# Issuing a retention-and-routing kernel in a hand-written order instead of by the automatic scheduler

## The chip, the cores and the metric

One Trainium2 chip, one of its cores. The metric is the device time of one execution in microseconds, lower is better. A core has TensorE (PE: matrix products and transposes into PSUM), VectorE (DVE), ScalarE (ACT), GpSimd (POOL), SyncE (SP, here only the issuer of transfers), and DMA engines that all of them share. Each engine runs its own instruction queue in order; semaphores between the queues carry the dependencies.

## The reference

Eight batches of eight-head retention (attention with a decay instead of a softmax) over 576 positions, then a layer in which each of the 4608 tokens goes to one of eight experts.

```python
def _attn_ref(q, k, v):                      # (8, 8, 576, 64) each
    scores = scale * np.matmul(q, k.transpose(0, 1, 3, 2))
    gamma = 1.0 - 2.0 ** (-5.0 - np.arange(H))
    Dmat = np.where(rel >= 0, gamma[:, None, None] ** rel[None], 0.0)   # rel = query - key position
    return np.matmul(scores * Dmat[None], v)

def _moe_ref(x, w_gate, w1, w2):             # x (4608, 512), w1 (8, 512, 1024), w2 (8, 1024, 512)
    logits = x @ w_gate
    expert_idx = np.argmax(logits, axis=1)
    gate_w = softmax(logits)[np.arange(N), expert_idx]
    for e in range(E):
        mask = expert_idx == e
        out[mask] = gate_w[mask, None] * (np.maximum(x[mask] @ w1[e], 0.0) @ w2[e])
```

## The kernel before

**Attention stage.** The work is cut into 40 blocks (`blocks`, a batch and a chunk): five per batch, four of 128 positions and a short one of 64. Decay is folded into q and k, so that a block needs only a causal mask, and what earlier chunks contribute is a running state. `load_batch` (L80) fetches q, k and v of a whole batch into tiles of two buffers. For each block TensorE does `stage_S` (L251: states from k and v), `stage_SC` (L281: scores, then the mask product `sc` on DVE, L305), `stage_R` of the block before (L356: transposes of the result back into rows, a cast `xr` on ACT, a store into the DRAM tensor `x_rows` by SP), `stage_TK` of the next block (L236: k scaled on POOL into `kk`, then transposed), `stage_AV` (L309: result into `psx`, copied out by ACT as `xo` and DVE as `xT`), and, one a block, `stage_TQ` for the next batch (L220: q scaled on POOL into `qq`, then transposed). `stage_L1` and `stage_L2` (L372, L386) make the routing logits once a batch.

**Routing.** `softmax_top1`, `ranks`, `prep`, `rows_hot` and `place` (L404 to L528) pick each token's expert, rank the tokens of each expert, and build lists of token numbers per expert (`slots`). They are mostly short DVE instructions. They run in two phases: phase 0 after half of the tokens, in the attention stage; phase 1 after all.

**Expert stage.** A unit is an expert and a phase: 256 token rows (two blocks of 128) in phase 0, 384 (three blocks) in phase 1. `seq` (L601) lists the 16 units. For a unit, `gather` (L530) has POOL issue an indirect transfer per block that reads rows of `x_rows` into `xg` (six buffers); `trans` (L605) transposes them; `mm1` (L616) multiplies with w1 into `ht`; `mm2` (L632) multiplies with w2, scales the result on DVE into `ys` (four buffers), and has POOL scatter a block of rows to the output by an indirect transfer (L643). All scatters write the one output tensor. Weights come as float32 in 512 KB parts, eight an expert, through three staging tiles `wst`, and are cast to bfloat16 by DVE or ACT (`load_w`, L199); an expert's weights have three buffers.

**Order.** The text traces the program in loops (L553 and L660). The automatic scheduler then orders each engine's instructions by a model of their times. Only TensorE's instructions are held to the text's order, by `pin` (L54), which `mm` (L58) uses too; POOL, DVE, ACT and SP get theirs from the scheduler. After the experts comes a branch for tokens that did not fit the lists; it isn't taken here.

Of the kernel before, what the change touches and what calls it, by code (L numbers as in the profile page):

```python
# [10 lines left out]
ALU = mybir.AluOpType  # L11
# [7 lines left out]
P = 128  # L19
# [19 lines left out]
def kernel(  # L39
# [14 lines left out]
    def pin(i):  # L54
        tc.keep_in_program_order(i)
        return i

    def mm(out, lhsT, rhs, start, stop):  # L58
        return pin(nc.tensor.matmul(out=out, lhsT=lhsT, rhs=rhs, start=start, stop=stop,  # L59
                                    skip_group_check=True))  # L60
# [7 lines left out]
    stpool = ctx.enter_context(tc.tile_pool(name="wstage", bufs=3))  # L68
# [4 lines left out]
    ldp = p1.enter_context(tc.tile_pool(name="ld", bufs=2))  # L73
    wkp = p1.enter_context(tc.tile_pool(name="wk", bufs=2))
    wk1 = p1.enter_context(tc.tile_pool(name="wk1", bufs=1))
    attc = p1.enter_context(tc.tile_pool(name="attc", bufs=1))
    ps1 = p1.enter_context(tc.tile_pool(name="ps1", bufs=1, space=PSUM))


    def load_batch(b, first):  # L80


        qt = ldp.tile([P, H, NCH, DH], F32, tag="q", name="qt")
        kt = ldp.tile([P, NCH, H, DH], F32, tag="k", name="kt")
        vt = ldp.tile([P, NCH, H, DH], F32, tag="v", name="vt")
        qk = ldp.tile([P, H, DH], F32, tag="qkr", name="qk")
        vr = ldp.tile([P, H // 2, DH], F32, tag="vr", name="vr")
        for c in range(NCH):
            nc.sync.dma_start(out=kt[:, c, :, :], in_=k[b, :, c * P:(c + 1) * P, :].rearrange("h p d -> p h d"))
            if first:  # L90
                nc.sync.dma_start(out=qt[:, 2 * c:2 * c + 2, :, :],
                                  in_=q[b, 2 * c:2 * c + 2, 0:NCH * P, :].rearrange("h (p s) d -> p h s d", p=P))
            elif c == 0:
                nc.sync.dma_start(out=qt[:, :, :, :],
                                  in_=q[b, :, 0:NCH * P, :].rearrange("h (p s) d -> p h s d", p=P))
            nc.sync.dma_start(out=vt[:, c, :, :], in_=v[b, :, c * P:(c + 1) * P, :].rearrange("h p d -> p h d"))
        nc.sync.dma_start(out=qk[0:REM, :, :], in_=q[b, :, NCH * P:S, :].rearrange("h p d -> p h d"))
        nc.sync.dma_start(out=qk[REM:P, :, :], in_=k[b, :, NCH * P:S, :].rearrange("h p d -> p h d"))
        for j in range(2):
            nc.sync.dma_start(out=vr[j * REM:(j + 1) * REM, :, :],  # L100
                              in_=v[b, 4 * j:4 * j + 4, NCH * P:S, :].rearrange("h p d -> p h d"))
        return qt, kt, vt, qk, vr

    loads = {0: load_batch(0, True)}
# [4 lines left out]

    tri = attc.tile([P, REM], F32, name="tri")  # L110
    nc.gpsimd.memset(tri[:, :], 1.0)
    for j in range(2):
        nc.gpsimd.affine_select(out=tri[j * REM:(j + 1) * REM, :], in_=tri[j * REM:(j + 1) * REM, :],
                                pattern=[[1, REM]], base=0, channel_multiplier=-1,
                                compare_op=ALU.is_ge, fill=0.0)
    wgp = attc.tile([P, NP, 32], F32, name="wgp")
    nc.gpsimd.memset(wgp[:, :, :], 0.0)
    nc.sync.dma_start(out=wgp[:, :, 0:E], in_=moe_w_gate.rearrange("(c p) e -> p c e", p=P))

# [33 lines left out]
    nc.vector.tensor_copy(out=kg[0:REM, NCH, :], in_=qg[0:REM, NCH, :])  # L153
    zst = attc.tile([P, NP, DH], F32, name="zst")
    nc.gpsimd.memset(zst[:, :, :], 0.0)
# [3 lines left out]
    pss = ps1.tile([P, 2, 512], F32, name="pss")  # L159

# [34 lines left out]

    wb = {}
    casts = [nc.scalar.copy, nc.vector.tensor_copy, nc.gpsimd.tensor_copy]

    def load_w(e, part, eng):  # L199

        if e not in wb:
            wb[e] = (wpool.tile([P, NPT, F], BF16, tag="w1", name="w1b"),
                     wpool.tile([P, NFB, DM], BF16, tag="w2", name="w2b"))
        w1b, w2b = wb[e]
        st = stpool.tile([P, F], F32, tag="st", name="wst")
        c = part % 4
        if part < 4:
            nc.sync.dma_start(out=st[:, :], in_=moe_w1[e, c * P:(c + 1) * P, :])
            casts[eng](out=w1b[:, c, :], in_=st[:, :])
        else:  # L210
            nc.sync.dma_start(out=st[:, :].rearrange("p (s d) -> p s d", d=DM),
                              in_=moe_w2[e, c * 2 * P:(c + 1) * 2 * P, :].rearrange("(s p) d -> p s d", p=P))
            casts[eng](out=w2b[:, 2 * c:2 * c + 2, :], in_=st[:, :].rearrange("p (s d) -> p s d", d=DM))  # L213

    qTs, kTs, kks, scs, sts, xTs, lts = {}, {}, {}, {}, {}, {}, {}

    def stage_TQ(b, p):  # L220

        qt = loads[b][0]
        h0 = 2 * p
        qq = wkp.tile([P, NCH, P], F32, tag="qq")
        nc.gpsimd.tensor_tensor(  # L225
            out=qq[:, :, :].rearrange("p s (h d) -> p h s d", d=DH), in0=qt[:, h0:h0 + 2, :, :],
            in1=qg[:, 0:NCH, h0:h0 + 2].rearrange("p s h -> p h s").unsqueeze(3)
                .to_broadcast([P, 2, NCH, DH]), op=ALU.mult)
        pst = ps1.tile([P, 512], F32, tag="T", name="psq")
        for s_ in range(NCH):  # L230
            pin(nc.tensor.transpose(out=pst[:, s_:512:NCH], in_=qq[:, s_, :], identity=ident[:, :]))  # L231
        if b not in qTs:
            qTs[b] = wkp.tile([P, NP, 512], F32, tag="qT", name="qT")
        nc.scalar.copy(out=qTs[b][:, p, :], in_=pst[:, :])

    def stage_TK(b, c):  # L236
        kt, qk = loads[b][1], loads[b][3]
        kk = wkp.tile([P, H, DH], F32, tag="kk")
        nc.gpsimd.tensor_tensor(out=kk[:, :, :], in0=(kt[:, c, :, :] if c < NCH else qk[:, :, :]),  # L239
                                in1=kg[:, c, :].unsqueeze(2).to_broadcast([P, H, DH]), op=ALU.mult)  # L240
        pst = ps1.tile([P, 512], F32, tag="T", name="psk")
        for p in range(NP):
            pin(nc.tensor.transpose(out=pst[:, p * P:(p + 1) * P],
                                    in_=kk[:, 2 * p:2 * p + 2, :].rearrange("p h d -> p (h d)"),
                                    identity=ident[:, :]))
        kT = wkp.tile([P, NP, P], F32, tag="kT")
        nc.scalar.copy(out=kT[:, :, :].rearrange("p a t -> p (a t)"), in_=pst[:, :])
        kTs[(b, c)] = kT
        kks[(b, c)] = kk

    def stage_S(b, c):  # L251

        if c == NCH:
            return
        kk, vt = kks.pop((b, c)), loads[b][2]
        for p in range(NP):
            for par in range(2):
                r = slice(par * DH, (par + 1) * DH)
                for j in range(2):
                    h = 2 * p + j  # L260
                    mm(pss[j * DH:(j + 1) * DH, par, p * DH:(p + 1) * DH], kk[r, h, :], vt[r, c, h, :],
                       c == 0 and p == 0, c == NCH - 1)
        so = wkp.tile([P, NP, DH], F32, tag="so")
        e_, o_ = pss[:, 0, 0:NP * DH], pss[:, 1, 0:NP * DH]
        fl = so[:, :, :].rearrange("p a d -> p (a d)")
        if c == 0:
            nc.vector.tensor_copy(out=fl, in_=e_)
        else:

            nc.vector.tensor_tensor(out=fl, in0=e_, in1=sts[(b, c, "oo")][:, :, :].rearrange("p a d -> p (a d)"),  # L270
                                    op=ALU.add)
        so2 = wkp.tile([P, NP, DH], F32, tag="so2")
        nc.scalar.copy(out=so2[:, :, :].rearrange("p a d -> p (a d)"), in_=o_)
        se = wkp.tile([P, NP, DH], F32, tag="se")
        nc.vector.tensor_tensor(out=se[:, :, :].rearrange("p a d -> p (a d)"), in0=e_,
                                in1=so2[:, :, :].rearrange("p a d -> p (a d)"), op=ALU.add)
        sts[(b, c, 1)] = so
        sts[(b, c + 1, "oo")] = so2
        sts[(b, c + 1, 0)] = se

    def stage_SC(b, c):  # L281
        kT = kTs.pop((b, c))
        ps = ps1.tile([P, 2, 512], F32, tag="SC", name="pssc")
        sc = wkp.tile([P, 2, NP, DH], F32, tag="sc")
        scs[(b, c)] = sc
        if c < NCH:
# [22 lines left out]
    def stage_AV(b, c):  # L309
# [37 lines left out]
        if c < NCH:  # L347
            if c == 0:
                xTs[b] = wk1.tile([P, NCH, NP, P], F32, tag="xT", name="xT")
# [434 lines left out]
```

## Time and profile before

| | |
|---|---|
| time, median of 14 runs | 468.58 us (463.47 to 476.95) |
| time of the profiled execution | 464.41 us |
| its span | 462.7 us, granted TensorE clock 0.925 |
| busy TensorE, VectorE, ScalarE, GpSimd | 346.0, 182.7, 175.6, 164.4 us |
| moved by DMA | 82.31 MB, 178 GB/s over the span |
| last transposes of the routing logits | 245.4 us |
| first and last scatter start | 256.2 and 449.8 us |

A span is what the profile covers of one execution, the time includes what lies around it. The busy tenths below are the span in 40 slices of 11.6 us: TensorE, POOL, the DMA engines, and what they moved in GB/s. The attention stage is the first 21 slices, the expert stage the rest.

```profile
PE   1678879897766778776867778989495978999700
...
POOL 7254332524233163231100364133325344643220
...
DMA  9988878988887597887010135998556674222110
GB/s 213 244 184 217 188 197 202 247 216 209 214 222 194 163 261 193 231 294 239 20 38 7 55 115 189 323 308 264 202 209 215 243 248 137 91 82 91 67 69 14
```

A timeline line has: start, duration, engine, line of the kernel, operation, what it writes and reads, how many of them; in square brackets, how long the engine had been idle before and what ended that. A line of the waits has: who waited for whom, total us, how often, the longest.

### The profile page before, as it was taken

The numbers are of one execution on the slowest core, as the hardware profiler recorded it, in microseconds if no ns is written. First come the engines' busy times: TensorE is split into PE (matmuls) and PEld (weight loads), VectorE is DVE, ScalarE is ACT, GpSimd is POOL, SyncE is SP. The second block draws the span as 40 slices with busy tenths as digits, with TensorE's granted clock in tenths as the row PEclk, the third lists the DMA queues.
The fourth block names the chain that finished last, engine by engine and source line by source line (L and its number), as shares of the span: only waits on it lengthen the run. The fifth ranks groups of instructions, "written<-read, shape, count | busy, mean of one in ns | idle before, by whom it ended". The sixth has DMA issues, their size and how long they took to land. (4 is left out here: it accounts for less than half of the span.)

```text
span 462.7 us, 14452 instructions
## 1 busy us (share of the span) xinstructions
PE 346.0 (75%) x6306; PEld 256.0 (55%) x6322; DVE 182.7 (39%) x436; ACT 175.6 (38%) x316; POOL 164.4 (36%) x198
## 2 busy tenths in 40 slices
PE   1678879897766778776867778989495978999700
PEld 1567768786656667665755544556254544656300
DVE  2134423433387933344448724444233324323200
ACT  2245434545563366564432014445142323232200
POOL 7254332524233163231100364133325344643220
PEclk9999989999999879998999799999798898999955
DMA  9988878988887597887010135998556674222110
GB/s 213 244 184 217 188 197 202 247 216 209 214 222 194 163 261 193 231 294 239 20 38 7 55 115 189 323 308 264 202 209 215 243 248 137 91 82 91 67 69 14
DMA packets 112008, 82.31 MB, mean 178 GB/s; under 512 B 83262, under 2 KB 96062, under 8 KB 111936
## 3 DMA queue, kind: packets, MB, share of 16 engines
q1 hardware_dynamic: 106816, 66.61, 51.7%
q0 software_dynamic: 5120, 14.69, 9.0%
q8 instruction: 51, 0.84, 0.7%
q14 instruction: 21, 0.17, 0.1%
HBM read 67.13 MB, written 15.20 MB: 178 GB/s over the span
## 5 line engine op out<-in xcount | busy, mean ns | idle before, releaser
L643 POOL DMA_INDIRECT out_dram<-ys,tids x40 | 42.5, 1062 | 126.0 <-issue 46.1
L629 ACT ACTIVATE ht<-pm 128x384 bf16<-128x384 f32 (+1 forms) x96 | 49.3, 526 | 91.1 <-PE pm L59 79.6
L59 PE MATMUL pm<-xt,w1b 128*128 128x256 bf16 (+1 forms) x512 | 75.0, 306 | 4.1 <-ACT ht L629 2.7
L59 PE MATMUL py<-w2b,ht 128*128 128x512 bf16 x304 | 73.0, 396 | 1.4 <-issue 0.7
L59 PEld LDWEIGHTS <-w1b 128*128 128x128 bf16 x512 | 51.3, 100 | 27.4 <-issue 4.9
L225 POOL TENSOR_TENSOR qq<-qt,qg 128x512 f32<-128x512 f32 x32 | 34.2, 1074 | 87.7 <-PE psq L231 60.9
L642 DVE TENSOR_SCALAR ys<-py,gat 128x512 f32<-128x512 f32 x40 | 29.8, 749 | 66.9 <-DMA out_dram<-ys,tids 40.8
L59 PEld LDWEIGHTS <-ht 128*128 128x128 bf16 x320 | 32.1, 102 | 37.9 <-issue 6.7
L239 POOL TENSOR_TENSOR kk<-kt,kg 128x512 f32<-128x512 f32 x32 | 33.6, 1050 | 49.2 <-issue 30.3
L536 POOL DMA_INDIRECT xg<-x_rows,tidg x40 | 41.6, 1041 | 19.1 <-issue 9.0
L354 DVE TENSOR_TENSOR xT<-psx,xo 128x512 f32<-128x512 f32 x32 | 22.1, 690 | 63.4 <-ACT xo L346 63.4
L346 ACT COPY xo<-psx 128x512 f32<-128x512 f32 (+1 forms) x40 | 21.8, 544 | 51.9 <-PE psx L59 51.9
L59 PE MATMUL psx<-sc,vt 64*64 64x64 f32 x1024 | 23.2, 230 | 18.2 <-DVE sc L305 15.9
L59 PE MATMUL psx<-qT,so 64*64 64x64 f32 x512 | 34.8, 225 | 2.1 <-issue 2.1
L231 PE MATMUL psq<-ident,qq 128*128 128x128 f32 x128 | 23.3, 309 | 14.5 <-POOL qq L225 13.2
L59 PEld LDWEIGHTS psx<-sc,vt 64*64 64x64 f32 x1024 | 18.8, 140 | 24.9 <-DVE sc L305 20.6
L366 PE MATMUL psr<-ident,xT 128*128 128x128 f32 x128 | 21.9, 295 | 12.6 <-DVE xT L354 12.6
L612 PE MATMUL pt<-identb,xg 128*128 128x128 bf16 x160 | 13.8, 225 | 22.4 <-DVE xt L613 19.3
L59 PEld LDWEIGHTS psx<-qT,so 64*64 64x64 f32 x512 | 29.3, 141 | 0.9 <-issue 0.9
L213 ACT CAST w2b<-wst 128x1024 bf16<-128x1024 f32 x16 | 16.7, 1048 | 33.0 <-DMA wst<-in_moe_w_dram 33.0
L368 ACT CAST xr<-psr 128x512 bf16<-128x512 f32 (+1 forms) x40 | 23.4, 584 | 15.3 <-PE psr L366 15.2
L59 PE MATMUL pss<-vt,kk 64*64 64x64 f32 x1024 | 25.6, 236 | 2.2 <-issue 2.1
(124 smaller groups left out, 519.6 us busy)
## 6 DMA issues: line engine op xcount, KB each, us to landing
wst<-in_moe_w_dram SPq DMA_DIRECT2D x64, 512.0 KB
kt<-in_k_dram SPq DMA_DIRECT2D x32, 256.0 KB
vt<-in_v_dram SPq DMA_DIRECT2D x32, 256.0 KB
qt<-in_q_dram SPq DMA_DIRECT2D x7, 1024.0 KB
x_rows<-xr SPq DMA_DIRECT2D x32, 128.0 KB
qt<-in_q_dram SPq DMA_DIRECT2D x4, 256.0 KB
qk<-in_q_dram SPq DMA_DIRECT2D x8, 128.0 KB
qk<-in_k_dram SPq DMA_DIRECT2D x8, 128.0 KB
```

The costliest lines, as they stand in the source:

```text
L59: return pin(nc.tensor.matmul(out=out, lhsT=lhsT, rhs=rhs, start=start, stop=stop, skip_group_check=True))
L225: nc.gpsimd.tensor_tensor(out=qq[:, :, :].rearrange("p s (h d) -> p h s d", d=DH), in0=qt[:, h0:h0 + 2, :, :], in1=qg[:, 0:NCH, h0:h0 + 2] ...
L231: pin(nc.tensor.transpose(out=pst[:, s_:512:NCH], in_=qq[:, s_, :], identity=ident[:, :]))
L239: nc.gpsimd.tensor_tensor(out=kk[:, :, :], in0=(kt[:, c, :, :] if c < NCH else qk[:, :, :]), in1=kg[:, c, :].unsqueeze(2).to_broadcast([P, ...
L346: nc.scalar.copy(out=xo[:, :], in_=psx[:, 1, 0:n * P])
L354: nc.vector.tensor_tensor(out=dst, in0=psx[:, 0, 0:n * P], in1=xo[:, :], op=ALU.add)
L366: pin(nc.tensor.transpose(out=ps[0:n, p * P:(p + 1) * P], in_=src, identity=ident[:, :]))
L368: nc.scalar.copy(out=xr[0:n, :], in_=ps[0:n, :])
L536: nc.gpsimd.indirect_dma_start(out=xg[:, :], out_offset=None, in_=x_rows[0:nr, :], in_offset=bass.IndirectOffsetOnAxis(ap=slots[ph][1][:, ...
L629: nc.scalar.activation(out=ht[:, f0:f0 + per, :], in_=pm[:, :, :], func=AF.Relu)
L642: nc.vector.tensor_scalar(out=ys[:, :], in0=py[:, :], scalar1=gat[:, i:i + 1], scalar2=None, op0=ALU.mult)
L643: nc.gpsimd.indirect_dma_start(out=out[:, :], out_offset=bass.IndirectOffsetOnAxis(ap=tids[:, i:i + 1], axis=0), in_=ys[:, :], in_offset=N ...
```

## The change

The scheduler is switched off (`manual_schedule`), `pin` goes, and every engine gets its instructions in the order of the text. The text is rewritten to be that order:

- k and v are loaded by block, with seven buffers each (`load_k`, `load_v`), q by batch; the loads stand in the loop seven blocks ahead.
- POOL's scaling is split from the transposes (`scale_q`, `scale_k`). An iteration issues: scaling of q for the next batch and of k three blocks ahead, scores of block i+1, transposes of k of i+2, states of i+1, rows of i−1, result of i, loads, transposes of q.
- One PSUM pool of two buffers (`psw`) serves all transposes instead of two of one.
- Routing functions yield after each DVE instruction; loops advance them by a few steps at a time.
- The units' order begins with three of phase 0 and three of phase 1. Loading and casting of weights are split (`load_w`, `cast_w`); in the expert stage there are six staging tiles, and three more experts' weights fit (`wpool2`).
- Casts go to DVE between matmul groups of `mm1`, to ACT after each block of `mm2`; each is followed by the next fetch.

The instructions and their sizes are otherwise the same, the casts moved between ACT and DVE apart. The core of the diff, with the new code as it stands where it replaces all of a part:

```diff
-    def pin(i):
-        tc.keep_in_program_order(i)
-        return i
+    ctx.enter_context(tc.manual_schedule())
...
-    ldp = p1.enter_context(tc.tile_pool(name="ld", bufs=2))
+    ldq = p1.enter_context(tc.tile_pool(name="ldq", bufs=2))
+    ldk = p1.enter_context(tc.tile_pool(name="ldk", bufs=7))
+    wk3 = p1.enter_context(tc.tile_pool(name="wk3", bufs=3))
+    psw = p1.enter_context(tc.tile_pool(name="psw", bufs=2, space=PSUM))
...
+    def steps(g, n):
+        for _ in range(n):
+            try:
+                next(g)
+            except StopIteration:
+                return False
+        return True
...
     for i, (b, c) in enumerate(blocks):
-        if c == 0 and b + 1 < B:
-            loads[b + 1] = load_batch(b + 1, False)
-        stage_S(b, c)
-        stage_SC(b, c)
+        if c < NP and b + 1 < B:
+            scale_q(b + 1, c)
+        scale_k(i + 3)
+        stage_SC(i + 1)
+        stage_TK(i + 2)
+        stage_S(i + 1)
         if i > 0:
-            stage_R(*blocks[i - 1])
-        if i + 1 < len(blocks):
-            stage_TK(*blocks[i + 1])
+            stage_R(i - 1)
         if c == 0 and b > 0:
             stage_L1(b - 1)
-        stage_AV(b, c)
+        stage_AV(i)
+        if i + 7 < NB:
+            load_k(i + 7)
+            load_v(i + 7)
+        if c == 4 and b + 2 < B:
+            load_q(b + 2, False)
         if c < NP and b + 1 < B:
             stage_TQ(b + 1, c)
         if c == 0 and b > 0:
             stage_L2(b - 1)
-        for (e, pt) in w_at.get(i, []):
-            load_w(e, pt, 0)
+        if i >= first_early and nearly < len(early):
+            load_w(*early[nearly], stpool)
+            nearly += 1
+        if len(staged) > 2 or (i == NB - 1):
+            while len(staged) > (2 if i < NB - 1 else 0):
+                cast_w("V")
...
+        if rf is not None:
+            steps(rf, 5)
+        if i == NB - 5:
+            while steps(rf, 1):
+                pass
             gather(0, 0)
             gather(1, 0)
+            gather(2, 0)
...
-    seq = [(0, 0), (1, 0), (0, 1), (1, 1)] + [(e, ph) for e in range(2, E) for ph in (0, 1)]
+    seq = [(e, 0) for e in range(3)] + [(e, 1) for e in range(3)] + [(e, ph) for e in range(3, E) for ph in (0, 1)]
...
+    rr = route_rest()
+    steps(rr, 12)
     trans(0, 0)
-    more_w(4)
-    incl1 = softmax_top1(1, rtm2)
+    fetch(6)
     for i, (e, ph) in enumerate(seq):
...
+        def during1():
+            if i < 3:
+                steps(rr, 6)
+            if i >= 1 and quota[0] > 0 and staged and (i >= 2 or len(staged) > 2):
+                cast_w("V")
+                fetch(1)
+                quota[0] -= 1
+
+        def during2():
+            if i < 3:
+                steps(rr, 8)
+            if staged:
+                cast_w("A")
+                fetch(1)
+
+        ht = mm1(e, ph, during1)
+        if nxt == (0, 1):
+            mm2(e, ph, ht, during2)
+            while steps(rr, 1):
+                pass
+            gather(0, 1)
+            gather(1, 1)
+            trans(*nxt)
+        else:
+            if nxt:
+                trans(*nxt)
+            mm2(e, ph, ht, during2)
+        if i >= 3 and i + 2 < len(seq):
             gather(*seq[i + 2])
-        more_w(4)
```

`mm1` calls `during1` after each group of matmuls and its activation, `mm2` calls `during2` after each block's scatter.

## The prediction

> **What bounds the kernel now.** I read the busy shares first, then the sums by stage, then the timelines of two places, then the waits. The page says only that no engine is the bound of the whole:
>
> ```profile
> PE 346.0 (75%) x6306; PEld 256.0 (55%) x6322; DVE 182.7 (39%) x436; ACT 175.6 (38%) x316; POOL 164.4 (36%) x198
> ```
>
> So the stages have to be read apart. The attention stage ends when the last logits are transposed, at 245.9 us; the first scatter follows at 256.2, the last matmul ends at 437, the span at 462.7. I call 245.9 the point P. Sums by stage (stretch, its length, busy time by engine, granted clock, DMA share, GB/s):
>
> ```profile
> 24.00:246.00 222.00, 174.87 (x5135) 151.71 (x5135) 102.26 (x258) 107.15 (x196) 72.09 (x69) 0.95 0.73 194
> 246.00:286.00 40.00, 31.14 (x219) 20.26 (x223) 21.58 (x79) 9.77 (x18) 16.65 (x16) 0.91 0.23 75
> 286.00:437.00 151.00, 129.93 (x802) 76.44 (x812) 53.24 (x90) 52.60 (x92) 59.25 (x57) 0.94 0.57 196
> ```
>
> In the attention stage TensorE is the busiest engine, and its gaps are the loss. One undisturbed block, from the timeline:
>
> ```profile
> 113.17 0.60 PE L243 MATMUL psk<-ident,kk 128*128 128x128 f32 x4
> 113.57 0.68 DVE L305 TENSOR_TENSOR sc<-pssc,tri 128x512 f32<-128x512 f32 x1
> 114.31 0.69 PE L59 MATMUL psx<-sc,vt 64*64 64x64 f32 x32 [0.54 <-DVE sc L305]
> ```
>
> TensorE computes scores, runs out of other work and waits 0.54 us for the mask. The block's period is 4.87 us (xT at 111.77 and 116.64).
>
> The expert stage is bound by no engine at all, but by a chain on POOL. Each scatter (L643) writes the same output tensor, and waits for the one before it to land:
>
> ```profile
> 299.79 1.28 POOL L643 DMA_INDIRECT out_dram<-ys,tids  x1 [5.52 <-DVE ys L642]
> 301.38 1.04 POOL L536 DMA_INDIRECT xg<-x_rows,tidg  x1 [0.30 <-PE pm L59]
> 302.73 1.01 POOL L536 DMA_INDIRECT xg<-x_rows,tidg  x1 [0.30 <-issue]
> 304.60 1.03 POOL L643 DMA_INDIRECT out_dram<-ys,tids  x1 [0.85 <-DVE w2b L213]
> ...
> 424.53 0.98 POOL L643 DMA_INDIRECT out_dram<-ys,tids  x1 [2.54 <-DMA out_dram<-ys,tids]
> 428.04 0.99 POOL L643 DMA_INDIRECT out_dram<-ys,tids  x1 [2.53 <-DMA out_dram<-ys,tids]
> ```
>
> From 286.65 to 449.82 there are 35 scatter periods, 4.66 us each: 3.5 us when no weights are loading, up to 6.5 us beside weight loads. Results wait for a place in this chain, not the chain for results:
>
> ```profile
> DVE ys L642 <- DMA out_dram<-ys,tids: 40.8, 14, 5.7
> ```
>
> Note the two gathers above: they sit inside a scatter's wait and cost nothing. The scheduler put them there, several units ahead of their use.
>
> **The change, attention stage.** The arithmetic is the same. What moves:
>
> Start. q is loaded before k and v of later blocks, and the first block's scaling needs no whole batch. The first xT, at 24.0 us now, was behind q pieces that arrived until 14.6. With 1.25 MB at the first stage's 223 GB/s (5.6 us), then four qq of 1.07 us each and the same PE work behind them, about 17.5: −6.5 us (bounds 0 and −8).
>
> Order of blocks. Scores of block i+1, transposes of i+2 and states of i+1 now stand before AV of block i, so the mask (0.68) and xo plus xT (0.59, 0.69) each have more than 1.5 us of TensorE work as cover. That removes 0.54 us in 32 regular blocks and the 0.46 us before R in 8 short ones: −21 us. Without this cover the gaps come back at that price.
>
> Disturbances. The 39 block intervals from 24.0 to 241.8 take 217.8 us; eight undisturbed batches (3×4.87+5.24+3.14=23.0) less the first block would take 181. The other 37 us are loads late by a batch (about 10), and routing, weight casts and a slowed clock in batches 4 to 6 (about 27). New: k and v come seven blocks ahead, and routing goes five DVE steps at a time. DVE then has so 0.42, se 0.42, sc 0.68, xT 0.69, a cast 0.69 and five steps of 0.35, together 4.65 us against 4.33 of TensorE, in some 14 blocks: 5 us stay. The rank and placement matmuls wait for DVE in TensorE's order: 5 us. On SP's queue each x_rows store and weight load stands before the next loads: 5 us. So −22 of 37 (bounds −37 and 0).
>
> P = 245.9−6.5−21−22 = 196. Lower bound 181. Upper bound 218: the 38.6 MB up to the last k and v (28.3 MB inputs, 4 MB x_rows, 6.3 MB weights) at 210 GB/s, the mean of the page's first 16 slices, are 184 us, then eight blocks (30) and the logits (4).
>
> **The change, expert stage.** Removed: the routing block on DVE between 251 and 263 that held up the chain (scatters 1 to 4 came only at 260, 275, 279 and 287). Added: order. On POOL the gathers of unit i+2 are now queued behind all scatters of unit i, each of which waits for the one before. Behind them waits TensorE: trans(i+1) stands before mm2(i), so mm2(i) waits for gathers that waited for the scatters of unit i−1, and only mm2(i) feeds the scatters of unit i. The chain, which was always full, becomes a circle. Its price from rows: the row of a late gather and its transposes
>
> ```profile
> 266.17 1.00 POOL L536 DMA_INDIRECT xg<-x_rows,tidg  x1 [0.30 <-PE pm L59]
> ...
> 269.80 0.40 PE L612 MATMUL pt<-identb,xg 128*128 128x128 bf16 x4 [1.10 <-DMA xg<-x_rows,tidg]
> ```
>
> gives 3.6 us from issue to use. From the last scatter of unit i−1 to the first of unit i: scatter issue 1.3, further gathers 1.3 each, 3.6, transposes 0.4, eight w2 matmuls 1.75, latency 0.2, ys 0.75, POOL 0.4: 11.0 us with three gathers, 9.7 with two. A narrow unit (2 scatters, three gathers next) takes 11.0+3.5, a wide one (3, two next) 9.7+7.0.
>
> TensorE idles 6 us and more before a narrow unit's transposes. The trace shows what follows: after 2.09 us of idle at 60 us (granted clock 0.91 in 60 to 80, 1.00 in 80 to 100) four transposes took 1.11 us, not 0.66, and 32 matmuls at 262 took 5.97, not 3.65. At ×1.7 the first eight w2 matmuls cost +1.2 (bounds 0 and 1.75). Narrow: 15.7. Together 32.4 us per expert, against 18 now (scatters 32 and 37: 424.53 to 442.83).
>
> The Trainium skill (TensorE: Matmul & The Clock Gate, "Why this matters for your kernels") puts the drop after an idle gap of about 3 us. The trace shows it after 2.09 us. By the page the wide units, idle about 2 us, stay at full clock, as in my sum; by the row they would lose 1.2 us each too, 6 us over the stage.
>
> Sum from P:
> - First scatter at +15.5 (10.3 now; 12 routing steps, about 3 us, stand before the first xt copy on DVE, 24 more before ys). Five periods at 5.5 beside 20 weight parts (10.5 MB at 320 GB/s, as in the stage's best slices: 33 us): +43 (bounds 33 and 48).
> - Unit 3: its six gathers stand behind these scatters: 7.5 to the third, xt 0.9, cold mm1 7.5 (5.36 warm), transposes 0.9, w2 and ys 3.1, two periods at 5: +30, so +73.
> - Units 4 and 5 beside weights: 11.0+2×5=21, 9.7+2×4.6=19: +113.
> - Units 6 to 13: four times 32.4, and 4 for the last weights: +247.
> - The last two: 12.2, then TensorE's own pace 9.6, then 7.0: +276.
> - End: 12.9 from the last scatter's start, as now: +289, against 216.8 now.
>
> Weights on SP: fetches now follow casts, six staging tiles ahead instead of three; 25 MB at 320 GB/s is 79 us, inside the 130 us that these units take, so they cost only the slower scatters counted above. If casts on DVE and ACT had to wait for them, up to 15 us more.
>
> **Sum.** 196+289 = 485 of span, 487 with the 1.7 us around it (464.4 for 462.7 now): +23. The median of the runs shown is 468.6, 0.9% above the profiled one, so I put 488.
>
> **Rivals.**
> - *DMA bounds the attention stage* (0.17). For it: a share of 0.73 on average and 1.05 in the first 24 us; batches 4 to 6 now want 6.75 MB in 22 us, 307 GB/s, and no slice of this stage went above 294. Against: seven blocks of lead. P=218: 218+289+2 = 509.
> - *The gathers do not wait behind the scatters* (0.13; the other side). Place: POOL's queue in the expert stage; that is so if the written order isn't what POOL gets, as where the change does not do what it says for this queue. Price: the circle is gone, the chain alone stays: first scatter +15.5, 39 periods of 4.6, end 12.9, +208; 196+208+2 = 406. It decides once transposes wait for xg under 1 us a unit. Against: every POOL row keeps one order, and the text now fixes it.
> - *Gain and loss cancel* (0.08): P at its bound 181, no cold matmuls (−6), first scatters at +33 (−10): 181+273+2 = 456; with half of that, 471.
>
> **How the numbers follow.** My forecast holds 0.62, with a range of its own of 466 to 505 (P ±12, expert stage ±15). 0.17 lie about 509, 0.13 about 406, 0.08 from 456 to 471. Leaving the 406 case out, 456 to 518 holds about 8 in 10. A measurement of this kernel tells about 0.5% from no change. Faster: 0.13, half of the cancelling case, and little of mine: 0.22. Same: 0.04. Slower: 0.74.
>
> **What would show it.** P near 196 and a regular block near 4.3 us; POOL rows in the order scatter, scatter, gathers; transposes pt waiting for DMA xg for some 50 us in all (2.2 now); DVE ys waiting for out_dram near zero (40.8 now); pairs of scatters 3.5 us apart with holes of 10 to 12; an expert in 31 to 34 us. I am wrong if scatters run at an even 3.5 to 6 us through the expert stage, or if P stays above 218.

## The result, and the profile after

The change makes the kernel slower: 570.37 us median of 10 runs (567.21 to 572.98), beside 468.62 us for the kernel before in the same comparison. The ratio is 1.2242, 95% interval 1.2204 to 1.2281. The profiled execution took 573.27 us, for a span of 571.5 us at a granted clock of 0.823. The prediction had 488 us and a range of 456 to 518: slower was right, the size was not, and the time lies far above the range. Ratios, and differences between kernels, are of the fast executions where some of a kernel's own are slower than the rest.

Two stretches make up the span, before and after the point P. In after and in all later kernels P is the start of the last transposes of the logits; in before that start is 245.4, and the prediction's 245.9 lies half a microsecond behind it.

| | before | predicted | after |
|---|---|---|---|
| first xT | 24.0 us | 17.5 | 18.6 |
| P | 245.9 | 196 | 271.1 |
| P to the end of the span | 216.8 | 289 | 300.4 |

So the expert stage, where the loss was forecast, is off by 11 us, and the attention stage, where a gain was forecast, by 75. The page of after, busy time by engine:

```profile
PE 390.0 (68%) x6306; PEld 271.8 (48%) x6322; DVE 200.7 (35%) x453; ACT 163.0 (29%) x301; POOL 162.7 (28%) x196
```

TensorE executes 6306 instructions as before, and is busy for 44 us more: it runs at a lower clock (0.823 against 0.925, and 346.0 times 0.925 over 0.823 is 389). The sums by stage of after (stretch, length, busy time of PE, PEld, DVE, ACT and POOL, granted clock, DMA share, GB/s):

```profile
19.00:271.00 252.00, 194.82 (x5066) 160.38 (x5066) 110.86 (x244) 89.19 (x175) 75.57 (x71) 0.86 0.59 154
271.00:320.00 49.00, 30.14 (x213) 20.30 (x217) 29.07 (x100) 13.13 (x19) 8.83 (x9) 0.81 0.67 249
320.00:559.00 239.00, 155.12 (x811) 83.43 (x821) 54.47 (x94) 53.64 (x95) 65.43 (x66) 0.79 0.33 113
```

In the attention stage the DMA share fell from 0.73 to 0.59 and the clock from 0.95 to 0.86: this is a stage that waits, not one that is short of bandwidth. In the waits of after, four lines have grown:

```profile
POOL out_dram L755 <- DVE ys L754: 106.5, 17, 11.3
POOL qq L219 <- DMA qt<-in_q_dram: 89.3, 5, 21.8
PE pt L60 <- DMA xg<-x_rows,tidg: 86.1, 30, 12.2
...
PE psq L60 <- POOL qq L219: 40.9, 8, 8.0
```

The third line is the circle of the expert stage: TensorE waits 86.1 us for gathered rows (2.2 before, some 50 predicted), and by the first line POOL's scatters wait for results (5.8 before), where before the results waited for the scatters. The second and the last line are what the prediction did not have: POOL waits for q (10.1 before; the view puts two more such waits, 37.5 us together, down to loads of v), and TensorE for POOL (13.2 before). The timeline of after at one such place, batch 3 being scaled:

```profile
75.19 0.66 SPq L93 DMA_DIRECT2D qt<-in_q_dram  x1
84.61 1.06 POOL L219 TENSOR_TENSOR qq<-qt,qg 128x512 f32<-128x512 f32 x1 [20.35 <-DMA qt<-in_q_dram]
85.62 1.04 POOL L229 TENSOR_TENSOR kk<-kt,kg 128x512 f32<-128x512 f32 x1
85.72 1.11 PE L60 MATMUL psq<-ident,qq 128*128 128x128 f32 x4 [7.96 <-POOL qq L219]
...
88.25 1.11 PE L60 MATMUL psk<-ident,kk 128*128 128x128 f32 x4
...
92.27 0.66 PE L60 MATMUL psq<-ident,qq 128*128 128x128 f32 x4
```

q is issued at 75.19, 9.4 us before its first use, and POOL stands at qq with the scaling of k, which has long been loaded, in order behind it. TensorE runs through what it has, then idles 7.96 us, and its next transposes take 1.11 us instead of 0.66. From the psr transposes at 90.12 on, four take 0.66 again. The intervals between xT of successive blocks, from the timeline, tell the same of all batches: the interval that ends at block (b,1) is 12.5, 12.4, 14.6, 13.2, 13.0, 12.8 and 14.8 us in the first seven batches, where it is 4.8 undisturbed. The other four of an undisturbed batch are 4.6, 3.7, 4.1 and 5.1, in sum 22.3.

The text of the kernel shows why. load_q(b+2) stands at c = 4 of batch b, the last block, and scale_q(b+2, 0) at c = 0 of batch b+1: the next block. The load of k stands four blocks ahead of the scaling that uses it. The page has the time from issue to landing as the last number of the row, and it is longer than a block:

```profile
qt<-in_q_dram SPq DMA_DIRECT2D x7, 1024.0 KB, 7.4
```

In the expert stage POOL's rows of after show the circle in the forecast order:

```profile
430.72 0.98 POOL L755 DMA_INDIRECT out_dram<-ys,tids  x1 [2.52 <-issue]
432.00 1.04 POOL L603 DMA_INDIRECT xg<-x_rows,tidg  x1 [0.30 <-issue]
433.35 1.01 POOL L603 DMA_INDIRECT xg<-x_rows,tidg  x1 [0.30 <-DMA out_dram<-ys,tids]
434.66 1.00 POOL L603 DMA_INDIRECT xg<-x_rows,tidg  x1 [0.30 <-issue]
442.74 1.03 POOL L755 DMA_INDIRECT out_dram<-ys,tids  x1 [7.08 <-DVE ys L754]
446.31 1.00 POOL L755 DMA_INDIRECT out_dram<-ys,tids  x1 [2.54 <-issue]
447.61 1.04 POOL L603 DMA_INDIRECT xg<-x_rows,tidg  x1 [0.30 <-PE pm L57]
448.95 1.01 POOL L603 DMA_INDIRECT xg<-x_rows,tidg  x1 [0.30 <-PE pm L57]
456.54 1.03 POOL L755 DMA_INDIRECT out_dram<-ys,tids  x1 [6.57 <-DVE ys L754]
```

The holes between scatters are 12.0 us with three gathers in them (430.72 to 442.74; 12.2 predicted with the cold clock) and 10.2 with two (446.31 to 456.54; 9.7 predicted). Whole experts, from the first scatter of a narrow unit to that of the next, take 33.7, 33.0, 32.1 and 32.9 us; 32.4 was predicted.

### The profile page after: what moved, and what is told of

Its sections match the earlier page's. It is cut to its first block, busy times and chain, and to the rows that moved or that the text cites. A ratio compares the mean times of both kernels' runs of the same rounds, so it can differ in the third digit from the quotient of the medians.

```text
span 571.5 us, 14550 instructions
## 1 busy us (share of the span) xinstructions
PE 390.0 (68%) x6306; PEld 271.8 (48%) x6322; DVE 200.7 (35%) x453; ACT 163.0 (29%) x301; POOL 162.7 (28%) x196
## 5 line engine op out<-in xcount | busy, mean ns | idle before, releaser
L57 PE MATMUL py<-w2b,ht 128*128 128x512 bf16 x304 | 87.2, 451 | 2.7 <-issue 2.4
L60 PE MATMUL pt<-identb,xg 128*128 128x128 bf16 x160 | 21.0, 281 | 86.5 <-DMA xg<-x_rows,tidg 86.1
L219 POOL TENSOR_TENSOR qq<-qt,qg 128x512 f32<-128x512 f32 x32 | 33.8, 1059 | 141.0 <-DMA qt<-in_q_dram 89.3
L724 DVE COPY xt<-pt 128x512 bf16<-128x512 bf16 x40 | 16.6, 422 | 129.1 <-PE pt L60 127.1
L60 PEld LDWEIGHTS <-xg 128*128 128x128 bf16 x160 | 12.9, 122 | 95.5 <-DMA xg<-x_rows,tidg 94.7
L229 POOL TENSOR_TENSOR kk<-kt,kg 128x512 f32<-128x512 f32 x40 | 43.6, 1097 | 17.7 <-issue 10.1
L60 PEld LDWEIGHTS psq<-ident,qq 128*128 128x128 f32 x128 | 16.4, 164 | 44.5 <-POOL qq L219 43.1
L60 PE MATMUL psk<-ident,kk 128*128 128x128 f32 x160 | 29.8, 315 | 9.2 <-POOL kk L229 7.3
L251 ACT COPY kT<-psk 128x512 f32<-128x512 f32 x40 | 23.6, 590 | 41.9 <-PE psk L60 38.8
L311 DVE TENSOR_TENSOR sc<-pssc,tri 128x512 f32<-128x512 f32 (+1 forms) x40 | 25.2, 630 | 21.2 <-PE pssc L57 19.8
L241 ACT COPY qT<-psq 128x512 f32<-128x512 f32 x32 | 18.9, 590 | 45.6 <-PE psq L60 45.6
```

The lines of the kernel that those rows point to most:

```text
L60: nc.tensor.transpose(out=out, in_=in_, identity=identity)
L219: nc.gpsimd.tensor_tensor(out=qq[:, :, :].rearrange("p s (h d) -> p h s d", d=DH), in0=qts[b][:, h0:h0 + 2, :, :], in1=qg[:, 0:NCH, h0:h0 ...
L229: nc.gpsimd.tensor_tensor(out=kk[:, :, :], in0=kts.pop(i)[:, :, :], in1=kg[:, blocks[i][1], :].unsqueeze(2).to_broadcast([P, H, DH]), op=A ...
L311: nc.vector.tensor_tensor(out=sc[:, :, 0:n, :], in0=ps[:, :, 0:n * DH].rearrange("p j (a i) -> p j a i", i=DH), in1=tri[:, :].unsqueeze(1) ...
```

## The experiments

Eight kernels, in two groups of four, each group on one chip with the kernel before timed beside it (467.13 us in the first group, 467.62 in the second). The last four are compared with both_early, which is in the first group. Two theories were to be told from their rivals: that q's late load alone makes the attention stage long, and that the place of the gathers behind the scatters alone makes the expert stage long.

**q_early.** q is issued four blocks earlier, nothing else is changed:

```
-        if c == 4 and b + 2 < B:
+        if c == 0 and b + 2 < B:
             load_q(b + 2, False)
```

> The changed kernel with one edit: q of batch b+2 is issued at chunk 0 of batch b instead of chunk 4, so four blocks earlier; its buffer is free by then. Theory (POOL waits for a q transfer that is issued one block before its first use): six of the seven stalls of about 9 us go (the one in batch 0 stays, its q is issued before the loop), the intervals of the second blocks of batches 1 to 6 fall from 12.4 to 14.8 us to about 4 to 5, the attention stage ends near 215 instead of 271 us, the time falls from 570 to about 515. Rival (q is late because the DMA engines are full with k and v seven blocks ahead): the wait moves to k or v and the stage still ends above 255 us, time above 555. Expert stage unchanged at about 300 us in both.

531.95 us (526.92 to 533.86), ratio 1.1418 (1.1297 to 1.1539). P is at 233.2, the expert stage at 295.6. The first (b,1) interval stays at 13.0 us, because q of batch 1 is loaded by the prologue, behind k and v of blocks 3 and 4; the others become 4.8, 4.8, 4.8, 5.1, 7.3 and 6.8. That settles the cause of these waits: the wait did not move to k or v, as it would if the DMA engines were full. But the gain is 38 us and not the 55 expected. The (b,1) intervals are 46.8 us shorter in all, since the six waits came to 52 us and two of the intervals kept some; the others are 10.1 us longer in all (8.0 and 9.8 us for two in batches 2 and 3 that took 4.6).

**gather_first.** In the expert stage the gathers of unit i+2 move ahead of the scatters of unit i:

```
             if nxt:
                 trans(*nxt)
+            if i >= 3 and i + 2 < len(seq):
+                gather(*seq[i + 2])
             mm2(e, ph, ht, during2)
-        if i >= 3 and i + 2 < len(seq):
-            gather(*seq[i + 2])
```

> The changed kernel with one edit: from the fourth unit on, the gathers of unit i+2 are issued before the second matmuls and scatters of unit i instead of after them, so that on POOL they stand ahead of the scatters that wait for each other. Theory (circle of scatters, gathers, transposes, second matmuls): transposes no longer wait for gathers, scatters run at 3.5 us apart without holes of 10 to 12 us, an expert takes 18 to 20 us instead of 32.5, the expert stage takes 225 to 235 us instead of 300, time about 500. Rival (casts of weights, now in the text's order on DVE and ACT, or the slow TensorE clock hold the stage up): units stay above 28 us per expert and the time falls by less than 25 us.

499.53 us (495.99 to 499.9), ratio 1.0708 (1.0616 to 1.08). P is at 272.7, as in after; the expert stage takes 225.4 us, inside what was expected. POOL's rows of this kernel:

```profile
425.90 0.98 POOL L755 DMA_INDIRECT out_dram<-ys,tids  x1 [2.50 <-issue]
427.18 1.04 POOL L603 DMA_INDIRECT xg<-x_rows,tidg  x1 [0.30 <-PE pm L57]
428.53 1.01 POOL L603 DMA_INDIRECT xg<-x_rows,tidg  x1 [0.30 <-issue]
429.85 1.03 POOL L755 DMA_INDIRECT out_dram<-ys,tids  x1 [0.30 <-issue]
433.44 1.00 POOL L755 DMA_INDIRECT out_dram<-ys,tids  x1 [2.57 <-issue]
```

TensorE's wait for gathered rows falls from 86.1 to 28.4 us. The two gathers now stand in the time in which the next scatter has to wait anyway: from 425.90 to 429.85 two scatters are 3.95 us apart, in place of a hole of 10 us. The same instructions in another order on one queue are worth 75 us of the expert stage.

**both_early.** Both edits, and load_q(1) ahead of k and v of blocks 3 and 4:

```
-    for i in range(1, 5):
+    load_k(1)
+    load_v(1)
+    load_k(2)
+    load_v(2)
+    load_q(1, False)
+    for i in range(3, 5):
         load_k(i)
         load_v(i)
...
-    load_q(1, False)
```

> Both edits together, and q of batch 1 issued before k and v of block 3 instead of after block 4's. Theory: the two losses are in different stages and add up: attention stage ends near 205, expert stage 225 to 235, time 430 to 445, below both the changed kernel and the kernel before. Rival (one bottleneck behind both, such as DMA): less than three quarters of the sum of the two single gains.

458.26 us (457.06 to 465.27), ratio 0.9836 (0.9761 to 0.9911): a little faster than before. P is at 231.2 and the expert stage takes 228.6 us. The expert stage is as expected, the attention stage (205) and so the time (430 to 445) are not. Against after the single edits gave 38 and 71 us, both 112; the change in the prologue, which the single edits had not, took the first (b,1) interval from 13 to 9.3 us. So the two losses add up, and together they are more than all of the 102 us that the change cost.

**text_order_scheduled.** The order by hand is given up except on TensorE; the automatic scheduler arranges the other engines, from the same new text:

```
-    ctx.enter_context(tc.manual_schedule())
+    def pin(i):
+        tc.keep_in_program_order(i)
+        return i
...
-        nc.tensor.matmul(out=out, lhsT=lhsT, rhs=rhs, start=start, stop=stop, skip_group_check=True)
+        pin(nc.tensor.matmul(out=out, lhsT=lhsT, rhs=rhs, start=start, stop=stop, skip_group_check=True))
```

and the same for the transposes.

> The changed kernel with the automatic scheduler on again: only TensorE is held to the text's order, as in the kernel before; all buffers, loops, loads by block and generators stay. Theory (what costs is the order on SP and POOL, not the new structure): the scheduler issues q loads as soon as a buffer is free and gathers ahead of scatters, both stalls go, time below 470. Rival (the new structure itself costs, for instance smaller loads or routing in steps): time above 540.

449.48 us (448.89 to 450.11), ratio 0.9663 (0.959 to 0.9736). P is at 235.0, the expert stage takes 212.1 us. The same text with TensorE's order as written is faster than before, so it is not the new order of the arithmetic that costs. POOL still waits 17.4 us for q here, against 89.3 in after. POOL's rows show what the scheduler did without being told:

```profile
376.29 0.98 POOL L757 DMA_INDIRECT out_dram<-ys,tids  x1 [2.83 <-DVE xt L726]
377.58 1.04 POOL L605 DMA_INDIRECT xg<-x_rows,tidg  x1 [0.30 <-issue]
378.92 1.01 POOL L605 DMA_INDIRECT xg<-x_rows,tidg  x1 [0.30 <-DMA out_dram<-ys,tids]
380.24 1.00 POOL L605 DMA_INDIRECT xg<-x_rows,tidg  x1 [0.31 <-PE py L59]
381.54 1.03 POOL L757 DMA_INDIRECT out_dram<-ys,tids  x1 [0.30 <-issue]
```

Three gathers fit between two scatters 5.2 us apart.

**The rest of the attention stage.** With q in time, P was still 35 us above the forecast of 196. The (b,1) interval of batch 0 is still 9.3 us, but the others are near those of q_early. The trace of both_early has three long stops, in the intervals that end at blocks (2,2), (3,2) and (4,2) (7.9, 10.0 and 9.7 us), and TensorE's rows there show no releaser:

```profile
75.62 0.56 PE L57 MATMUL pss<-vt,kk 64*64 64x64 f32 x20
78.11 0.45 PE L57 MATMUL pss<-vt,kk 64*64 64x64 f32 x12 [1.93 <-issue]
...
103.56 0.26 PE L57 MATMUL pssc<-qT,kT 64*64 64x64 f32 x1 [2.59 <-issue]
103.75 1.11 PE L60 MATMUL psk<-ident,kk 128*128 128x128 f32 x4
```

One group of 32 like matmuls stops after the twentieth, for 1.93 us; the second stop comes before the last matmul of a pssc group, and the third, of 2.09 us, ends at 130.9. In each case the packet records show a 16 KB packet of the instruction queue that is late: it begins at 75.82, 100.90 and 128.61, 6.8 to 7.2 us after the one before it (mostly 3 to 6 elsewhere; one 7.3 us after the one before it, right behind the second stop, and one 9.6 us after, at 210.2, come without such a stop), some 5 to 7 us after q was issued as one load of 1 MB, and TensorE goes on 2.3 to 2.7 us later.

**q_in_pieces** (both_early, and q loaded as four pieces of 256 KB, one per block):

```
-        if c == 0 and b + 2 < B:
-            load_q(b + 2, False)
+        if c < NP and b + 2 < B:
+            load_q_piece(b + 2, c)
```

> Kernel both_early with one change: q of batch b+2 is loaded in four pieces of 256 KB, one at each of the blocks c=0..3 of batch b, instead of 1 MB in one issue at c=0. Question: what are the three long stops inside the blocks (2,2), (3,2) and (4,2) of both_early (excess 3.3, 5.4 and 5.1 us, each with a TensorE gap of 1.9 to 2.6 us behind no semaphore, some 5 to 7 us after the 1 MB load was issued, while a late 16 KB packet of the instruction queue began)? Theory (the instruction fetch comes late behind the burst of q): without the burst these three stops go, the end of the attention stage moves from 231 to about 218, kernel about 446 us. Rival (the fetch costs this at fixed places in the program, whatever the load, or at random): the stops stay, at these or other blocks, kernel within 3 us of 458.

449.83 us (447.76 to 452.3), ratio 0.9692 (0.9615 to 0.977). P is at 218.4, the expert stage unchanged at 227.6. The three intervals are 4.9, 4.6 and 6.1 us. Other traces repeat it: casts_on_act and six_gathers_first, which load q as 1 MB too, have a stop in each of the same three intervals (1.93, 2.10 and 2.10 us; 2.47, 2.86 and 1.55), and all of these end 2.3 to 2.8 us after a packet of the instruction queue began. With q in pieces two shorter stops are left, of 1.34 us ending at 125.3 and of 1.77 us at 142.5, as long behind packets that came 5.1 and 5.5 us after the ones before them. So the stops at the three blocks go with the burst, or all but the 1.34 us in the last of them, and stops as such do not need it. That the fetch is the link rests on the times of the packets alone.

**casts_on_act** (both_early, and the early weight casts on ScalarE):

```
-                cast_w("V")
+                cast_w("A")
```

> Kernel both_early with one change: the weight casts of the attention stage (one per block in batches 4 to 7) run on ScalarE instead of VectorE. Question: is VectorE's load what is left of the disturbances in batches 4 to 6 (block intervals of 5.9 to 7.2 us instead of 3.7 to 5.1)? Theory (yes): VectorE loses some 0.85 us per block of 4.65, these intervals shrink by about 0.8 us each, the stage ends 6 to 10 us earlier, kernel about 450 us. Rival (the rank and placement matmuls and the chain of routing steps set these intervals, or ScalarE becomes what VectorE was): within 3 us of 458, or slower.

454.27 us (450.55 to 461.2), ratio 0.977 (0.9661 to 0.9879): the interval overlaps that of both_early, and the gain of 5.4 us lies between the two expectations. In the trace the nine intervals that end at blocks (5,1) to (6,4) sum to 46.8 us instead of 50.3, a gain of 3.5 us, under half of what the theory gave them. The profiled P is 7.5 us earlier, but 6.1 of it is one interval, ending at (7,0), that is 4.9 us here and 11.0 in both_early; in six_gathers_first, whose casts are on VectorE, it is 5.9. The casts are at most a small part of what is left.

**six_gathers_first** (both_early, and the gathers of units 3 and 4 ahead of unit 2's scatters):

```
+            while steps(rr, 1):
+                pass
+            gather(0, 1)
+            gather(1, 1)
             mm2(e, ph, ht, during2)
-            while steps(rr, 1):
-                pass
-            gather(0, 1)
-            gather(1, 1)
             trans(*nxt)
```

> Kernel both_early with one change: the rest of the routing and the gathers of units 3 and 4 stand before the two scatters of unit 2 on POOL instead of behind them. Theory (the 20 us hole between the scatters of unit 2 and of unit 3 is the same wait behind scatters as in the other units): the hole shrinks to about 12 us, kernel about 450 us. Rival (routing on VectorE, not the scatters, holds these gathers back): the scatters of unit 2 come later by what the hole loses, kernel within 3 us of 458.

448.21 us (447.35 to 451.64), ratio 0.9664 (0.9579 to 0.9749). The hole ahead of unit 3's first scatter goes from 20.2 to 8.6 us, further than expected, and the scatters ahead of it come no later for it; the expert stage takes 216.2 us instead of 228.6.

**all_edits** (the three together).

> Kernel both_early with the three changes of q_in_pieces, casts_on_act and six_gathers_first together. If the three are separate waits, as the theories say, their gains add up: 13 + 8 + 8 us, kernel about 430 us. If only their rivals hold, within 5 us of 458.

437.48 us (435.74 to 437.89), ratio 0.9398 (0.9327 to 0.947), the fastest kernel of the study. The single edits gave 8.3, 5.4 and 9.9 us, together 23.6; all three give 20.6, most of the sum. It is less than the 29 us of the expectation because q's pieces and the casts gave less than the 13 and 8 us put there, and the gathers little more than their 8. Its sums by stage:

```profile
19.00:215.00 196.00, 174.63 (x5065) 145.03 (x5065) 97.44 (x228) 103.26 (x191) 74.27 (x71) 1.00 0.78 197
215.00:263.00 48.00, 34.17 (x228) 22.10 (x232) 32.14 (x107) 13.41 (x20) 11.17 (x11) 0.84 0.73 264
263.00:423.00 160.00, 131.84 (x795) 75.22 (x805) 51.46 (x88) 53.50 (x95) 63.28 (x62) 0.93 0.47 166
```

The attention stage does the work of after in 196 us instead of 252, with TensorE busy 89% of it at full granted clock.

## Why the prediction was right on one stage and wrong on the other

*Expert stage: the mechanism and the size were right.* The circle is there, and removing its cause alone (gather_first) takes 75 us off the stage. Of the sum from P, the first scatter came at +17.0 (predicted +15.5), s5 at +44.4 (+43), unit 3's last at +79.5 (+73), unit 4's last at +104.7 (+94), unit 5's last at +126.3 (+113), unit 13's last at +257.5 (+247), the last scatter at +287.8 (+276). The whole error of 11 us was made up to unit 5, where routing and weight loads lie beside the circle; the regular units after it took what was forecast or a little less. The slow clock of +1.2 us was right for narrow units: from 405 us on their first eight w2 matmuls take 2.6 to 3.4 us, where they take 1.73 in gather_first. But the wide units, which the sum kept at full clock, are as slow (2.8 to 3.4 us), behind waits of 1.4 to 2.2 us and then 0.9 to 1.0; the prediction's reading by the row of 2.09 us held, and not the one by a gap of about 3 us. TensorE's wait for gathered rows, forecast at some 50 us, was 86: 39 of it lie ahead of 390 us, in waits of up to 12.2, and the 47 behind that are what was forecast.

*Attention stage: the step that failed* is "−22 of 37 (bounds −37 and 0)", with the sentence that "k and v come seven blocks ahead" as its ground. The lead of q was never worked out: it was one block, against 7.4 us from issue to landing and a queue on POOL in which k's scaling stands behind q's. Neither bound held this case, for both were made of disturbances that the trace of before had. Nor did the upper bound of 218 for P, which was bytes over bandwidth: the first rival (*DMA bounds the attention stage*) asked whether enough arrives in all, not whether one load arrives in time, and after moves only 154 GB/s there.

The 39 block intervals of after sum to 248.2 us, and they split as follows. Seven undisturbed batches of 22.3 and the last four intervals (4.3, 3.8, 3.6 and 2.7) are 170.5. The seven waits for q add 59.7 (93.3 less seven times 4.8). The other 18 are disturbances, where 15 were forecast. So of the error of 75 us some 60 come from q's load, and 10.5 from the forecast of 160 us for the undisturbed batches. Of these 10.5, two are a slip in the prediction's sum: eight batches of 23.0 less the interval of 5.24 that the last one lacks are 178.7, not 181, so that 39 us and not 37 were disturbances. The rest is the term "−21 us" for the gaps.

*The gaps: right mechanism, size off.* It gave 8.2 us of the 21 (178.7 to 170.5). The sums over one batch of five blocks, first before, then both_early:

```profile
76.22:99.97 23.75, 20.91 (x659) 18.34 (x658) 9.57 (x21) 11.73 (x24) 9.37 (x10) 1.00 0.89 227
```

```profile
51.97:74.60 22.63, 22.41 (x670) 18.74 (x668) 9.94 (x21) 11.84 (x24) 9.38 (x9) 1.00 0.70 171
```

TensorE was idle for 2.84 us of the batch and is now idle for 0.22: the gaps went, as forecast. But its busy time grew by 1.5 us for the same work, at the same granted clock. By the starts of the groups, 32 pss matmuls took 0.51 us until the next group began and now take 0.63, four psr transposes 0.49 and now 0.57; the other groups kept theirs. Over four pss and five psr groups that is 0.9 of the 1.5 us. The order of neighbours on TensorE has changed too, and the starts show which neighbours go with the price. In both kernels alike four psq transposes (128*128) take 0.49 us when the next group is 128*128 too, and mostly 0.59 when it is 64*64. The groups that became dearer stood before a group of their own form and now stand before one of the other; the order of a regular block now changes form six times instead of four. Five psk groups of both_early that stand before psr, the same form, take 0.64 at the median and do not fit; no run changed the form of a neighbour alone.

*Some disturbances were only hidden.* In both_early, with most of the waits gone, the intervals sum to 209.6, 39 above the undisturbed 170.5, as many as in the kernel before (39); 4.5 of them are in the first (b,1) interval. q_in_pieces has 26, all_edits 23. After had 18 beside its waits. That loads and fetches caught up while TensorE stood still for q would explain it, but no run shows it by itself. Of what all_edits still has above the 15 that were forecast, no cause was settled.

*Smaller points.* The start was right: first xT at 18.6 for 17.5. The second rival (*the gathers do not wait behind the scatters*) fell for the kernel as changed, where the hand order is what POOL gets; where it does hold, its chain is right in kind and 4 to 17 us short in size (208 us forecast, 212.1 in text_order_scheduled, 225.4 in gather_first). *Gain and loss cancel* fell with P. The scatter periods of before beside weight loads, read as up to 6.5 us, went up to 7.5 once (330.2 to 337.7).

## What to carry to other kernels

When an order is fixed by hand, work out for every load the lead from its issue to its first use, in time, and what stands in order behind that use; q needed 7.4 us to land and had one block, and 1 MB in one issue then hurt elsewhere until it was cut into pieces. On an engine that issues transfers, put what others wait for (gathers) ahead of what only has to be finished (scatters that wait for one another): that order alone was worth 75 us here. And price the waits of a stage together, because a large one hides smaller ones that appear when it is gone.

## What the runs showed of the hardware

TensorE stopped for 1.9 to 2.6 us within a run of like matmuls, with no semaphore behind it, while a 16 KB packet of the instruction queue began late, 5 to 7 us after a load of 1 MB was issued (both_early at 75.82, 100.90 and 128.61). The trace of before has such a stop as well: 2.09 us at 60, where such a packet began at 59.91. That the packet holds TensorE up is a reading of the times. The Trainium skill (Runtime: NRT & Kernel Launch, "Instruction fetch mechanics") holds that crossing a 16 KiB boundary of the instruction stream is mostly hidden; most packets here do pass unseen, in agreement with that, but the three intervals of both_early with such a stop took 27.6 us together, and 15.6 with q in pieces.

After such a stop the matmuls slow down as after a wait: the four psk transposes at 103.75, behind a gap of 2.59 us, took 1.11 us instead of 0.66.
